# First channel product of the last batch: seven half-size products for eight in each pair of tiles, and the second half of u computed earlier

## The chip, the cores and the metric

The kernel runs on one core of a Trainium2 chip. The metric is the device time of one execution in microseconds; the kernel before has a median of 253.27 us over three runs (252.99 to 253.75). The core's engines are PE (matmuls, with PEld for its weight loads), DVE, ACT and POOL (elementwise work) and SP (which only issues DMAs). Each of them takes its instructions strictly in the order in which they stand in its queue, apart from weight loads on PE, and waits on semaphores for what other engines have to deliver.

## The reference

Attention over a window of 128 positions and 4 sink positions gives x; a residual MLP with affine steps follows. There are 4 batches, 8 heads, 768 positions, 64 elements per head, so x has 512 channels (`DM`), and the inner width `DFF` is 2048.

```python
scores = scale * q @ k.T                 # kept where pos < 4 or 0 <= i - j < 128
x      = softmax(scores) @ v             # heads side by side: 768 x 512 per batch
a1  = alpha1 * x + beta1
tok = w_tok @ a1                         # mixes the 768 positions
u   = x + lam * tok
a2  = alpha2 * u + beta2
out = u + lam * (relu(a2 @ w_ch1) @ w_ch2)
```

The "first channel product" is `a2 @ w_ch1` with its relu, the "second" is `relu(...) @ w_ch2`.

## The kernel before

The work is a list of some thousand tasks. Each task has a function that issues a few instructions on one engine, the tasks it comes after, and the buffers it uses. Nothing is decided while the kernel runs: three tables written into the source give the order in which the tasks are issued (`ORDER`, task numbers), the engine of each (`ENGINES`: 0 ACT, 1 DVE, 2 PE, 3 POOL, 4 SP) and the place of each buffer (`HOMES`). Waits follow from the data and from the reuse of buffers: a task that writes a buffer waits for the last reader of what lay there before.

```python
for i in order:
    t = self.tasks[i]
    e = (ACT, DVE, PE, POOL, SP)[int(engines[i])]
    ...
    t.fn(e)
```

The four batches overlap: while the channel products of batch b run on PE, the attention of batch b+1 is woven in between. The steps that the change touches, with the profile's lines:

- `tok` (L860) multiplies the token weights `wtokT` with `xh`, six tiles of 128 positions per batch (`tok3_0` to `tok3_5` for the last batch), six matmuls each. DVE adds the result to x (L867), giving u; ACT or POOL casts u to half precision (L155, L157); SP issues a transposing DMA for each tile (`uTx`, L919), and an affine step per 128 channels and half of the positions makes a2 transposed, `uT` (L884 on ACT, L886 on DVE).
- `mlp1` (L940) is the first channel product: for each half of the positions (`chk`, 384 of them) and each of 16 tiles of 128 inner channels, four matmuls 128x384 accumulate in one bank of PSUM, and a relu takes it to `hT` in half precision (L946 on ACT, L948 on DVE). In names, `h2_0_7` is batch 2, half 0, tile 7. Per batch that makes 128 matmuls and 32 relus.
- The second channel product of batches 1 to 3 (`prod`, L1057) is done as seven half-size products for eight, P1 to P7, each of three row tiles and eight matmuls 128x256 per tile; P2, P3 and P4 go on top of P1, P5 and P7 in the same banks, and in the names of trace and program they carry those names (a second piece `P5_2_0` is P3). `h_sums` (S1 to S4, L998 to L1001) makes sums and differences of `hT` on DVE in place, `w2_sums` (L972) those of the weights. DVE adds the products to x (L1070, L1088, L1093, L1096; two of the last two kinds also on POOL), after which rows are stored.
- PSUM has four single banks for `h`, `tok` and the P products (kind "d") and two double banks for attention scores (kind "S"). The pieces above therefore take turns in four banks: the next product in a bank waits until DVE or ACT has read what was there.
- In the stretch that the change uses for its new sums (about 150 to 168 us), PE does the last products of batch 1, the first `h2_0_x` tiles of batch 2, and the first scores of batch 3's attention. DVE has x additions, relus and mask multiplications (`E<-E,mask`, L662); POOL has casts of v (`vfs<-vnat`) and a masking select (L587).

```python
a = add(p, {PE: 651}, mm,
        [done["uT", b, chk, c] for c in range(NC)] + [done["w1", fi // 4]],
        [ph, bu])
done["h", b, chk, fi] = add(p + 0.1, {ACT: 395, DVE: 480}, relu, [a], [ph, bh])
```

Of the kernel before, what the change touches and what calls it, by code (L numbers as in the profile page):

```python
# [77 lines left out]
def kernel(  # L78
# [74 lines left out]
    def copy(e, o, i):  # L153
        if e == ACT:
            nc.scalar.copy(o, i)  # L155
        else:
            engine[e].tensor_copy(o, i)  # L157
# [774 lines left out]
    def mlp1(p, b, chk, fi):  # L932
        if fi == 0:
            hT[b, chk] = Buf("hT", None, None, f"hT{b}_{chk}")
        bh, bu = hT[b, chk], uT[b, 0]
        ph = Buf("d", [P, NTOK], FP32, f"h{b}_{chk}_{fi}")

        def mm(e):
            for c in range(NC):
                nc.tensor.matmul(  # L940
                    ph.t, w1f[:, c, fi * P : (fi + 1) * P],
                    bu.t[:, c, chk * NTOK : (chk + 1) * NTOK], start=(c == 0), stop=(c == NC - 1))

        def relu(e):
            if e == ACT:
                nc.scalar.activation(bh.t[:, fi, :], ph.t, AF.Relu)  # L946
            else:
                nc.vector.tensor_scalar_max(bh.t[:, fi, :], ph.t, 0.0)  # L948
# [385 lines left out]
```

## Time and profile before

| what | value |
|---|---|
| median of three runs | 253.27 us (252.99 to 253.75) |
| profiled execution: its own time | 253.3 us |
| profiled execution: span | 251.5 us |
| busy: PE, DVE, ACT, POOL | 245.2, 193.7, 131.5, 107.9 us |
| PE clock granted | 1.00 in every stretch that was read |

The span runs from the first to the last instruction of the profiled execution; 1.8 us of its time lie around the span. Busy time is the time in which an engine had an instruction running. A row of a timeline gives the start, the length, the engine, the source line, the operation, out<-in with buffer names (numbers left out) and shapes, the count xN of instructions drawn together, and in brackets the idle time ahead of it with what ended it.

### The profile page before, as it was taken

The page shows a single profiled execution, that of the slowest core. Times are in us where ns is not written, and L with a number is a line of the kernel's source. Part 1 is how long each engine was busy: PE and PEld are TensorE (multiplying, and loading weights), DVE is VectorE, ACT ScalarE, POOL GpSimd, SP SyncE. Part 2 cuts the span into 40 slices and gives each one's busy share as a digit, 9 for nine tenths or more (in the row PEclk, how much of TensorE's full clock was granted, in tenths as well). Part 3 has the DMA queues.
Part 4 walks back from the last instruction along what each step waited for, and adds up shares of the span by engine and source line. Part 5 has one row for each costly group of instructions (what it writes and reads, how often), then busy time and mean ns, then how long its engine had stood idle before and what let it go on. Part 6 is the DMA issues. An engine that isn't in the chain of part 4 may idle for free.

```text
span 251.5 us, 5513 instructions
## 1 busy us (share of the span) xinstructions
PE 245.2 (98%) x2167; PEld 160.2 (64%) x2167; DVE 193.7 (77%) x401; ACT 131.5 (52%) x218; POOL 107.9 (43%) x126
## 2 busy tenths in 40 slices
PE   8899999999999999999999999999999999999994
PEld 7654655575555444566777676567677676567883
DVE  6898987778788976688889995677689985119883
ACT  2389935788985125687750545556660235543000
POOL 8728724986866516442872040065563130000010
PEclk9999999999999999999999999999999999999999
DMA  6999999999999997796489264420000147100006
GB/s 206 212 262 346 222 183 292 361 357 285 219 208 220 231 198 163 166 257 150 108 171 183 55 148 136 126 65 0 3 0 3 21 77 234 46 0 3 22 3 229
DMA packets 86129, 38.79 MB, mean 154 GB/s; under 512 B 73540, under 2 KB 80460, under 8 KB 86104
## 3 DMA queue, kind: packets, MB, share of 16 engines
q1 hardware_dynamic: 66976, 28.85, 48.2%
q10 hardware_dynamic: 15384, 6.32, 10.5%
q0 software_dynamic: 3744, 3.28, 8.3%
q8 instruction: 17, 0.28, 0.5%
q14 instruction: 8, 0.07, 0.1%
HBM read 29.91 MB, written 6.29 MB: 144 GB/s over the span
## 4 chain that ended last, share of the span: by engine, by line
PE 90%; ACT 4%; DVE 3%; issue 1%; DVEq 0%; ACTq 0%
PE h L940 32%; PE P L1057 22%; PE tok L860 12%; PE ch L1125 8%; PE pv L726 4%; PE S L625 4%; PE idle L148 2%; PE tp L515 1%; ACT wt L822 1%; ACT E L647 1%; DVE qkT L157 1%; PE S L620 1%; PE tp L512 1%; PE pv L719 1%; DVE lb_b L1175 1%
## 5 line engine op out<-in xcount | busy, mean ns | idle before, releaser
L940 PE MATMUL h<-uT,w1f 128*128 128x384 f16 x512 | 89.3, 326 | 0.1
L940 PEld LDWEIGHTS <-w1f 128*128 128x128 f16 x512 | 48.4, 98 | 31.9 <-issue 2.0
L946 ACT ACTIVATE hT<-h 128x384 f16<-128x384 f32 x77 | 36.7, 492 | 34.5 <-PE h L940 30.7
L948 DVE TENSOR_SCALAR hT<-h 128x384 f16<-128x384 f32 x51 | 27.4, 552 | 23.7 <-PE h L940 23.3
L1057 PEld LDWEIGHTS <-hT 128*128 128x128 f16 x408 | 39.3, 98 | 7.2 <-DVE hT L1000 0.7
L647 ACT ACTIVATE E<-S 128x1024 f16<-128x1024 f32 (+1 forms) x39 | 37.9, 1002 | 6.8 <-PE S L625 5.7
L770 POOL TENSOR_TENSOR tm<-x,la_b 128x512 f32<-128x512 f32 x18 | 24.7, 1372 | 22.2 <-DVE xh L773 12.0
L860 PE MATMUL tok<-xh,wtokT 128*128 128x512 f16 x144 | 33.2, 379 | 0.0
L1057 PE MATMUL P<-w2f,hT 128*128 128x256 f16 x216 | 26.8, 273 | 0.0
L155 ACT CAST u<-x 128x512 f16<-128x512 f32 x17 | 10.3, 616 | 28.3 <-DVE x L867 27.3
L1093 POOL TENSOR_TENSOR x<-x,pt 128x256 f32<-128x256 f32 x4 | 3.8, 961 | 46.0 <-DVE pt L1088 46.0
L1070 DVE TENSOR_TENSOR x<-x,P 128x256 f32<-128x256 f32 x45 | 18.0, 417 | 6.8 <-PE P L1057 6.0
L1057 PE MATMUL P<-w2s,hT 128*128 128x256 f16 x192 | 23.3, 273 | 0.0
L860 PEld LDWEIGHTS <-wtokT 128*128 128x128 f16 x144 | 13.8, 98 | 14.8 <-issue 0.2
L1125 PE MATMUL ch<-w2f,hT 128*128 128x512 f16 x96 | 22.7, 379 | 0.0
L752 DVE TENSOR_TENSOR x<-pv,rec 128x256 f32<-128x256 f32 x48 | 20.4, 425 | 1.7
L155 ACT CAST n<-nat 128x768 f16<-128x768 f32 x20 | 16.2, 830 | 7.9 <-DMA out_dram<-x 4.8
L867 DVE TENSOR_TENSOR x<-x,tok 128x512 f32<-128x512 f32 x24 | 16.0, 681 | 4.5 <-PE tok L860 4.3
L726 PEld LDWEIGHTS <-E 128*128 128x128 f16 x328 | 15.2, 97 | 4.9 <-issue 1.1
L726 PE MATMUL pv<-vfs,E 128*128 128x65 f16 x328 | 17.7, 193 | 0.0
L587 POOL TENSOR_SCALAR_AFFINE_SELECT E<-E 128x512 f16<-128x512 f16 x12 | 8.8, 753 | 17.9 <-ACT E L647 17.9
L157 POOL CAST vfs<-vnat 128x512 f16<-128x512 f32 x18 | 13.5, 752 | 4.3 <-PE pv L726 4.2
(133 smaller groups left out, 340.1 us busy)
## 6 DMA issues: line engine op xcount, KB each, us to landing
wst_w<-in_moe_w_ch_dram SPq DMA_DIRECT2D x8, 512.0 KB, 7.4
nat<-in_q_dram SPq DMA_DIRECT2D x10, 384.0 KB, 4.3
nat<-in_k_dram SPq DMA_DIRECT2D x10, 384.0 KB, 8.1
vnat<-in_v_dram SPq DMA_DIRECT2D x14, 256.0 KB, 6.2
out_dram<-x SPq DMA_DIRECT2D x12, 256.0 KB, 3.4
wtn<-in_moe_w_tok_dram SPq DMA_DIRECT2D x6, 384.0 KB, 4.8
out_dram<-x ACTq DMA_DIRECT2D x9, 256.0 KB, 4.3
w1f<-in_moe_w_ch_dram POOLq DMA_DIRECT2D x4, 512.0 KB, 10.2
```

Of the source, the lines that this page charges most:

```text
L155: nc.scalar.copy(o, i)
L647: nc.scalar.activation(eT.t, pS.t[:, :, 0 : n * w].rearrange("p e (i w) -> p e i w", i=n), AF.Exp, scale=scale)
L726: nc.tensor.matmul(po.t[:, hl, :], eT.t[:, e_, off + i, c : c + P], vf[j][:, h, :], start=(r < 2 and n == 0), stop=(n == len(parts) - 1 an ...
L752: nc.vector.tensor_mul(bx.t[:, 4 * G : 4 * G + 4, :], po.t[:, :, 0:D], rec.t.to_broadcast([P, 4, D]))
L770: engine[e].tensor_mul(bt.t, bx.t.rearrange("p h d -> p (h d)"), la1_b)
L860: nc.tensor.matmul(bank(), wtokT[:, si, ti * P : (ti + 1) * P], hs[si].t, start=(si == 0), stop=(si == NR - 1))
L940: nc.tensor.matmul(ph.t, w1f[:, c, fi * P : (fi + 1) * P], bu.t[:, c, chk * NTOK : (chk + 1) * NTOK], start=(c == 0), stop=(c == NC - 1))
L946: nc.scalar.activation(bh.t[:, fi, :], ph.t, AF.Relu)
L948: nc.vector.tensor_scalar_max(bh.t[:, fi, :], ph.t, 0.0)
L1057: nc.tensor.matmul(pc.t, hh[:, nt * P : (nt + 1) * P], w(fi), start=(first and n_ == 0), stop=(n_ == HF - 1), skip_group_check=True)
L1070: nc.vector.tensor_add(row(bx)[:, cols], row(bx)[:, cols], pc.t)
L1125: nc.tensor.matmul(pc.t, bh.t[:, fi, nt * P : (nt + 1) * P], w2f[:, fi, :], start=(fi == 0), stop=(fi == NF - 1))
```

## The change

For batch 3 alone, `mlp1` is replaced by `mlp1_pair`, which is called for i = 0 to 7 and makes inner tiles i and i+8 for both halves of the positions together. The four blocks (two inner tiles by two halves of the positions, with the 512 channels cut in two) are had from seven half-size products P1 to P7 of two matmuls 128x384 each, 14 for the former 16. Three kinds of additions come with it:

- `w1_sums`: sums and differences aS1 to aS4 of quarters of `w_ch1`, each in two halves of 128x2x512 in half precision. They are independent of the data and are placed in the stretch 150 to 168 us, five on POOL and three on DVE.
- `u_sums`: T1 to T4, differences of quarters of `uT` (128x768), T1, T3 and T4 on POOL, T2 on DVE.
- per pair, a copy of P1 from one PSUM bank to another (k1), the relu r11, copies of P6 and P5 to SBUF (k2 and k5, `hU` and `hV`), two additions of a PSUM bank and a copy (a22, a12), the relu r21, and two relus in place in SBUF (`clip`), one on POOL and one on DVE on average: seven passes over PSUM and two clips for the former four passes.

`hA` are the two double banks, which are free of scores by then. For the second half of u, `tok3_3`, `tok3_4` and `tok3_5` are issued ahead of batch 2's products P6, P5 and P3; `tok3_3` and `tok3_4` go to the double banks. The casts, transposes and affine steps behind them move with them.

```diff
-        601, 741, 765, 742, 771, 766, 760, 916, 772, 746, 751, 917, 773, 752, 913, 886,
+        601, 741, 765, 742, 771, 986, 766, 760, 916, 772, 746, 751, 917, 773, 987, 752,
...
-        pt = Buf("S" if (b, ti) == (0, 5) else "d", None, None, f"tok{b}_{ti}")
+        pt = Buf("S" if (b, ti) in ((0, 5), (3, 3), (3, 4)) else "d", None, None, f"tok{b}_{ti}")
...
+    HPAIR = (3,)
+    def w1_sums(p):
+        a11, a12 = w1f[:, 0:2, 0 : DFF // 2], w1f[:, 2:4, 0 : DFF // 2]
+        a21, a22 = w1f[:, 0:2, DFF // 2 : DFF], w1f[:, 2:4, DFF // 2 : DFF]
+        for s in ("S1", "S2", "S3", "S4"):
+            aS[s] = Buf("wst", [P, 2, DFF // 2], FP16, f"w1{s}")
+        for s, sub_, i0, i1, need in (("S1", 0, a21, a22, None), ("S2", 1, "S1", a11, "S1"),
+                                      ("S3", 1, a11, a21, None), ("S4", 1, a12, "S2", "S2")):
+            for g in range(2):
+                f = slice(512 * g, 512 * g + 512)
...
+                    op = engine[e].tensor_sub if sub_ else engine[e].tensor_add
+                    op(aS[s].t[:, :, f], r0[:, :, f], r1[:, :, f])
...
+    def u_sums(p, b):
...
+        for s, i0, i1, need, parts in (("T1", b12, b11, None, c11 + c12), ("T2", b22, "T1", "T1", c22),
+                                       ("T3", b22, b12, None, c12 + c22), ("T4", b21, "T2", "T2", c21)):
...
+                engine[e].tensor_sub(uD[b, s].t, r0, r1)
...
+    def mlp1_pair(p, b, i):
...
+        k_ = i + NF // 2
+        bA = pairs[b, i % 4 // 2]
+        bB = Buf("d", [P, NTOK], FP32, f"hB{b}_{i}")
+        bE = Buf("d", [P, NTOK], FP32, f"hE{b}_{i}")
+        bU = Buf("E", [P, NTOK], FP32, f"hU{b}_{i}")
+        bV = Buf("E", [P, NTOK], FP32, f"hV{b}_{i}")
...
+        m1 = mm("P1", A, lambda n_: w(n_, i), lambda n_: tok_(n_, 0), True, True, w1_ + half, [bA, bu])
+        k1 = add(p, {ACT: 395, DVE: 480}, lambda e, k=f"k1.{i}": copy(e, bB.t, A()), [m1], [bA, bB])
+        m2 = mm("P2", B_, lambda n_: w(2 + n_, i), lambda n_: tok_(2 + n_, 0), False, True, w1_ + half + [k1], [bB, bu])
+        done["h", b, 0, i] = relu("r11", c11, B_, [m2], [bB, h0])
+        m6 = mm("P6", A, lambda n_: sums("S2", n_), lambda n_: uD[b, "T2"].t[:, n_], False, True,
...
+        k2 = add(p, {ACT: 395, DVE: 480}, lambda e, k=f"k2.{i}": copy(e, bU.t, A()), [m6], [bA, bU])
+        m5 = mm("P5", E_, lambda n_: sums("S1", n_), lambda n_: uD[b, "T1"].t[:, n_], True, True,
...
+        m7 = mm("P7", A, lambda n_: sums("S3", n_), lambda n_: uD[b, "T3"].t[:, n_], False, True,
...
+        k5 = add(p, {ACT: 395, DVE: 480}, lambda e, k=f"k5.{i}": copy(e, bV.t, bE.t), [m5], [bE, bV])
+        a22 = plus("a22", c22, A, lambda: bV.t, [m7, k5], [bV, bA, h1])
+        done["h", b, 1, k_] = clip("r22", c22, [a22], [h1])
+        m4 = mm("P4", A, lambda n_: w(2 + n_, k_), lambda n_: uD[b, "T4"].t[:, n_], False, True,
...
+        done["h", b, 0, k_] = relu("r21", c21, A, [m4], [bA, h0])
+        m3 = mm("P3", E_, lambda n_: sums("S4", n_), lambda n_: tok_(2 + n_, 1), False, True,
...
+        a12 = plus("a12", c12, E_, lambda: bU.t, [m3, k2], [bE, bU, h1])
+        done["h", b, 1, i] = clip("r12", c12, [a12], [h1])
...
+        if b in HPAIR:
+            m1 = [("us",)] + [("hp", i) for i in range(NF // 2)]
```

The lines of the functions move: in the changed kernel L981 are the sums of `w_ch1`, L1001 those of `uT`, L1031 the matmuls of a pair, L1044 and L1046 its relus, L1051 the additions, L1056 the clips; L867 is `tok`, L955 DVE's relu of `mlp1`, L669 the mask multiplication, L1202 an addition of a product to x, L1225 and L1228 those from `pt`, L1189 the second channel product.

What the tables do to the queues is seen in the order of the instructions. POOL, at about 150 us, before the change: the last x addition of batch 1 there, a cast of v, the select on batch 3's first scores, more casts.

```order
L1093 TENSOR_TENSOR x1_2_1308<-x1_2_1308,pt1_2_2193 128x256
L157 CAST vfs_98<-vnat3_4_2269 128x8x64
L587 AFFINE_SELECT E3_1_0_2684<-E3_1_0_2684 128x4x128 x2
L157 CAST vfs_98<-vnat3_2_2204 128x8x64
L157 CAST vfs_98<-vnat3_1_2599 128x8x64
```

And in the changed kernel:

```order
L1225 TENSOR_TENSOR x1_2_1308<-x1_2_1308,pt1_2_2193 128x256
L157 CAST vfs_98<-vnat3_4_2269 128x8x64
L981 TENSOR_TENSOR w1S1_2694<-w1f_107 128x2x512
L981 TENSOR_TENSOR w1S2_2696<-w1S1_2694,w1f_107 128x2x512
L981 TENSOR_TENSOR w1S1_2694<-w1f_107 128x2x512
L981 TENSOR_TENSOR w1S2_2696<-w1S1_2694,w1f_107 128x2x512
L981 TENSOR_TENSOR w1S4_2700<-w1f_107,w1S2_2696 128x2x512
L594 AFFINE_SELECT E3_1_0_2687<-E3_1_0_2687 128x4x128 x2
L157 CAST vfs_98<-vnat3_2_2204 128x8x64
```

Five sums now stand between the cast and the select; S2 reads S1, and S4 reads S2, half by half.

DVE in the same stretch, before the change: the last x additions of batch 1 from `pt1` and from the products P5, then the relus of batch 2 with a mask multiplication between.

```order
L1093 TENSOR_TENSOR x1_0_1370<-x1_0_1370,pt1_0_2304 128x256
L1070 TENSOR_TENSOR x1_0_1370<-x1_0_1370,P5_1_0_2496 128x256
L1096 TENSOR_TENSOR x1_4_1530<-x1_4_1530,pt1_1_2181 128x512
L1070 TENSOR_TENSOR x1_4_1530<-x1_4_1530,P5_1_1_2532 128x256
L948 TENSOR_SCALAR hT2_0_2554<-h2_0_7_2559 128x384
L948 TENSOR_SCALAR hT2_0_2554<-h2_0_4_2549 128x384
L948 TENSOR_SCALAR hT2_0_2554<-h2_0_0_2584 128x384
L948 TENSOR_SCALAR hT2_0_2554<-h2_0_11_2591 128x384
L662 TENSOR_TENSOR E3_0_0_2589<-E3_0_0_2589,mask0_80 128x1024
L948 TENSOR_SCALAR hT2_0_2554<-h2_0_5_2601 128x384
```

And in the changed kernel:

```order
L1225 TENSOR_TENSOR x1_0_1370<-x1_0_1370,pt1_0_2304 128x256
L1202 TENSOR_TENSOR x1_0_1370<-x1_0_1370,P5_1_0_2496 128x256
L1228 TENSOR_TENSOR x1_4_1530<-x1_4_1530,pt1_1_2181 128x512
L1202 TENSOR_TENSOR x1_4_1530<-x1_4_1530,P5_1_1_2532 128x256
L981 TENSOR_TENSOR w1S3_2570<-w1f_107 128x2x512
L955 TENSOR_SCALAR hT2_0_2554<-h2_0_7_2559 128x384
L955 TENSOR_SCALAR hT2_0_2554<-h2_0_4_2549 128x384
L981 TENSOR_TENSOR w1S3_2570<-w1f_107 128x2x512
L955 TENSOR_SCALAR hT2_0_2554<-h2_0_0_2586 128x384
L955 TENSOR_SCALAR hT2_0_2554<-h2_0_11_2593 128x384
L669 TENSOR_TENSOR E3_0_0_2591<-E3_0_0_2591,mask0_80 128x1024
L955 TENSOR_SCALAR hT2_0_2554<-h2_0_5_2604 128x384
```

The two halves of S3 stand in front of the relus of `h2_0_7` and `h2_0_0`. (The second half of S4 goes to DVE too, between the relu of `h2_0_15` and the reciprocal `rec3_0_0`, some dozen rows later.) In this stretch everything else has kept its order on both engines.

PE, the first matmul of each group from `tok3_2` on (at about 195 us), before the change:

```order
L860 MATMUL tok3_2_3193<-xh3_0_2832,wtokT_106 128x512
L1057 MATMUL P6_2_0_3201<-w2s0_1491,hT2_0_2554 128x256
L1057 MATMUL P6_2_1_3228<-w2s0_1491,hT2_0_2554 128x256
L860 MATMUL tok3_4_3240<-xh3_0_2832,wtokT_106 128x512
L860 MATMUL tok3_3_3250<-xh3_0_2832,wtokT_106 128x512
L1057 MATMUL P5_2_0_3263<-w2s0_1491,hT2_1_2884 128x256
L860 MATMUL tok3_5_3273<-xh3_0_2832,wtokT_106 128x512
L940 MATMUL h3_0_1_3333<-uT3_3237,w1f_107 128x384
```

And in the changed kernel, up to the second product that uses a T sum:

```order
L867 MATMUL tok3_2_3204<-xh3_0_2844,wtokT_106 128x512
L867 MATMUL tok3_3_3216<-xh3_0_2844,wtokT_106 128x512
L867 MATMUL tok3_4_3228<-xh3_0_2844,wtokT_106 128x512
L867 MATMUL tok3_5_3240<-xh3_0_2844,wtokT_106 128x512
L1189 MATMUL P6_2_1_3254<-w2s0_1491,hT2_0_2554 128x256
L1189 MATMUL P6_2_2_3264<-w2s0_1491,hT2_0_2554 128x256
L1031 MATMUL hA3_1_3305<-uT3_3213,w1f_107 128x384
L1031 MATMUL hB3_0_3322<-uT3_3213,w1f_107 128x384
L1031 MATMUL hE3_0_3390<-uD3T1_3344,w1S1_2694 128x384
L1031 MATMUL hB3_1_3375<-uT3_3213,w1f_107 128x384
L1031 MATMUL hA3_0_3309<-uD3T2_3373,w1S2_2696 128x384
```

The token products `tok3_3` to `tok3_5` have moved ahead of P6 of batch 2, and where `h3_0_1` opened the first channel product, products of the pairs stand between batch 2's last products, first those that need no sum. Ahead of `tok3_3` PE's queue is unchanged.

More of the change, by code (lines that the diff above doesn't have):

```diff
@@ L953, in mlp1, with f_ @@
         done["h", b, chk, fi] = add(p + 0.1, {ACT: 395, DVE: 480}, relu, [a], [ph, bh])
+    HPAIR = (3,)
+    aS = {}
+    uD = {}
+    pairs = {}
+    def w1_sums(p):
[7 more added lines that the diff above has]
+                f = slice(512 * g, 512 * g + 512)
+                def f_(e, s=s, sub_=sub_, i0=i0, i1=i1, f=f):
+                    r0, r1 = [aS[z].t if isinstance(z, str) else z for z in (i0, i1)]
+                    op = engine[e].tensor_sub if sub_ else engine[e].tensor_add
+                    op(aS[s].t[:, :, f], r0[:, :, f], r1[:, :, f])
+                done["a" + s, g] = add(
+                    p, {POOL: 2500, DVE: 700}, f_,
+                    [done["w1", i] for i in range(4)] + ([done["a" + need, g]] if need else []),
+                    [aS[s]] + ([aS[need]] if need else []), port=True)
@@ new lines, in mlp1_pair, with mm, f_, tok_ @@
+    def mlp1_pair(p, b, i):
+        bu = uT[b, 0]
+        if i == 0:
+            for chk in range(2):
+                hT[b, chk] = Buf("hT", None, None, f"hT{b}_{chk}")
+            for g in range(2):
+                pairs[b, g] = Buf("S", None, None, f"hA{b}_{g}")
+        h0, h1 = hT[b, 0], hT[b, 1]
+        k_ = i + NF // 2
[4 more added lines that the diff above has]
+        bV = Buf("E", [P, NTOK], FP32, f"hV{b}_{i}")
+        A = lambda: bA.t[:, i % 2, 0:NTOK]
+        w = lambda c, f: w1f[:, c, f * P : (f + 1) * P]
+        g = i // 4
+        def mm(name, o, ws, xs, start, stop, after, uses):
+            def f_(e, name=f"{name}.{i}"):
+                for n_ in range(2):
+                    nc.tensor.matmul(o(), ws(n_), xs(n_), start=start and n_ == 0, stop=n_ == 1,
+                                     skip_group_check=True)
+            return add(p, {PE: 326}, f_, after, uses)
+        def tok_(c, chk):
+            return bu.t[:, c, chk * NTOK : (chk + 1) * NTOK]
+        def sums(s, n_):
+            return aS[s].t[:, n_, i * P : (i + 1) * P]
+        def relu(name, o, pt, after, uses):
+            def f_(e, name=f"{name}.{i}"):
+                if e == ACT:
+                    nc.scalar.activation(o(), pt(), AF.Relu)
+                else:
+                    nc.vector.tensor_scalar_max(o(), pt(), 0.0)
+            return add(p, {ACT: 395, DVE: 480}, f_, after, uses)
+        def plus(name, o, i0, i1, after, uses):
+            def f_(e, name=f"{name}.{i}"):
+                nc.vector.tensor_add(o(), i0(), i1())
+            return add(p, {DVE: 480}, f_, after, uses)
+        def clip(name, o, after, uses):
+            def f_(e, name=f"{name}.{i}"):
+                engine[e].tensor_scalar_max(o(), o(), 0.0)
+            return add(p, {POOL: 600, DVE: 250}, f_, after, uses, port=True)
+        w1_ = [done["w1", z] for z in range(4)]
+        B_ = lambda: bB.t
+        E_ = lambda: bE.t
+        c11, c21 = (lambda: h0.t[:, i, :]), (lambda: h0.t[:, k_, :])
+        c12, c22 = (lambda: h1.t[:, i, :]), (lambda: h1.t[:, k_, :])
+        half = [done["uT", b, 0, c] for c in range(NC)]
+        m1 = mm("P1", A, lambda n_: w(n_, i), lambda n_: tok_(n_, 0), True, True, w1_ + half, [bA, bu])
[3 more added lines that the diff above has]
+        m6 = mm("P6", A, lambda n_: sums("S2", n_), lambda n_: uD[b, "T2"].t[:, n_], False, True,
+                [k1, done["aS2", g], done["uT2", b]], [bA, aS["S2"], uD[b, "T2"]])
+        k2 = add(p, {ACT: 395, DVE: 480}, lambda e, k=f"k2.{i}": copy(e, bU.t, A()), [m6], [bA, bU])
+        m5 = mm("P5", E_, lambda n_: sums("S1", n_), lambda n_: uD[b, "T1"].t[:, n_], True, True,
+                [done["aS1", g], done["uT1", b]], [bE, aS["S1"], uD[b, "T1"]])
+        m7 = mm("P7", A, lambda n_: sums("S3", n_), lambda n_: uD[b, "T3"].t[:, n_], False, True,
+                [k2, done["aS3", g], done["uT3", b]], [bA, aS["S3"], uD[b, "T3"]])
+        k5 = add(p, {ACT: 395, DVE: 480}, lambda e, k=f"k5.{i}": copy(e, bV.t, bE.t), [m5], [bE, bV])
+        a22 = plus("a22", c22, A, lambda: bV.t, [m7, k5], [bV, bA, h1])
+        done["h", b, 1, k_] = clip("r22", c22, [a22], [h1])
+        m4 = mm("P4", A, lambda n_: w(2 + n_, k_), lambda n_: uD[b, "T4"].t[:, n_], False, True,
+                w1_ + [a22, done["uT4", b]], [bA, uD[b, "T4"]])
+        done["h", b, 0, k_] = relu("r21", c21, A, [m4], [bA, h0])
+        m3 = mm("P3", E_, lambda n_: sums("S4", n_), lambda n_: tok_(2 + n_, 1), False, True,
+                [k5, done["aS4", g]] + [done["uT", b, 1, c] for c in range(NC)], [bE, aS["S4"], bu])
+        a12 = plus("a12", c12, E_, lambda: bU.t, [m3, k2], [bE, bU, h1])
+        done["h", b, 1, i] = clip("r12", c12, [a12], [h1])
@@ L1230 @@
             seq += two("P1", "P2")
-            i = seq.index(("m1", 1, 8))
+            i = seq.index(("pr", "P1", 0) if b in HPAIR else ("m1", 1, 8))
             seq[i:i] = [("hs", "S3")]
@@ L1261 @@
                 p -= PAR["p7"]
-            {"tok": tok, "uT": uTp, "m1": mlp1, "m2": mlp2, "hs": h_sums, "pr": prod}[what](p, b, *args)
+            {"tok": tok, "uT": uTp, "m1": mlp1, "m2": mlp2, "hs": h_sums, "pr": prod,
+             "us": u_sums, "hp": mlp1_pair}[what](p, b, *args)
             if b and what == "tok":
```

26 lines of the change are left out of this document (21 added, 5 removed), and 56 rows, old and new, of the table ORDER.

## The prediction

> **What bounds the kernel now.** I read the engine totals first, then the chain of waits, then the busy time by stretches, and last the timelines of the engines around the places where the change puts work.
>
> ```profile
> span 251.5 us, 5513 instructions
> PE 245.2 (98%) x2167; PEld 160.2 (64%) x2167; DVE 193.7 (77%) x401; ACT 131.5 (52%) x218; POOL 107.9 (43%) x126
> PE 90%; ACT 4%; DVE 3%; issue 1%; DVEq 0%; ACTq 0%
> L940 PE MATMUL h<-uT,w1f 128*128 128x384 f16 x512 | 89.3, 326 | 0.1
> 152.26 2.60 PE h L940 x16
> ...
> 155.40 4.66 PE h L940 x28
> ...
> 210.10 18.85 PE h L940 x116
> 228.95 1.75 PE P L1057 x16
> ...
> 247.98 0.42 DVE x L1070
> ```
>
> PE is busy for 245.2 of 251.5 us, and 90% of the chain that ended last is PE's. The chain's own rows give the real pace: 116 first-product matmuls in 18.85 us are 0.1625 us each (the 326 ns of the group row is a length with overlap).
>
> ```profile
> 150.00:155.00 5.00, 5.00 (x40) 3.43 (x39) 3.25 (x8) 1.19 (x3) 0.43 (x1) 1.00 0.48 166
> 155.00:160.00 5.00, 5.00 (x38) 2.78 (x35) 3.98 (x8) 2.62 (x5) 0.00 (x0) 1.00 0.68 175
> ...
> 215.00:220.00 5.00, 5.00 (x32) 3.01 (x31) 0.56 (x1) 3.40 (x9) 0.00 (x0) 1.00 0.14 52
> 220.00:225.00 5.00, 5.00 (x33) 3.03 (x31) 1.12 (x2) 2.61 (x6) 0.00 (x0) 1.00 0.00 0
> ```
>
> After the stretch come busy PE, weight loads, DVE, ACT and POOL, then PE's granted clock. PE is busy 5.00 of 5 us both where the weight sums go (150 to 165) and where the pairs go (215 to 225), at a clock of 1.00. So a matmul taken away is worth its full time, and a wait put on PE costs its full time too. Between those ends the other engines look free: POOL did nothing from 155 to 160.
>
> **Part 1: fewer matmuls.** 128 become 112, so 16 × 0.1625 = 2.6 us less on the path. That is certain as PE work; only waits can eat it. **−2.6.**
>
> **Part 2: five weight sums on POOL.** They fill this hole:
>
> ```profile
> 149.80 0.64 POOL L157 CAST vfs<-vnat 128x512 f16<-128x512 f32 x1
> 163.86 1.22 POOL L587 TENSOR_SCALAR_AFFINE_SELECT E<-E 128x512 f16<-128x512 f16 x2 [13.43 <-ACT E L647]
> ...
> 96.25 1.16 POOL L972 TENSOR_TENSOR w2s<-w2f,w2s 128x512 f16<-128x512 f16 x1
> 97.36 1.16 POOL L972 TENSOR_TENSOR w2f<-w2f 128x512 f16<-128x512 f16 x1
> ```
>
> Two sums of half the size start 1.11 us apart, so one of 1024 elements per partition takes about 2.15 us (2 × 1.16 = 2.32 above, and less if part of 1.16 is fixed). Five are 10.8 us, and the hole is 13.43. Counted by POOL alone they cost nothing. [...]
>
> But other rows show what a running POOL instruction does to DVE.
>
> ```profile
> 97.75 1.32 DVE L662 TENSOR_TENSOR E<-E,mask 128x1024 f16<-128x1024 f16 x1
> 157.31 0.68 DVE L662 TENSOR_TENSOR E<-E,mask 128x1024 f16<-128x1024 f16 x1
> 189.49 1.27 POOL L770 TENSOR_TENSOR tm<-x,la_b 128x512 f32<-128x512 f32 x1
> 189.85 1.72 DVE L999 TENSOR_TENSOR hT<-hT 128x1536 f16<-128x1536 f16 x1
> 185.99 0.95 DVE L998 TENSOR_TENSOR hS<-hT,hT 128x1536 f16<-128x1536 f16 x1
> 186.22 1.84 POOL L770 TENSOR_TENSOR tm<-x,la_b 128x512 f32<-128x512 f32 x1 [0.50 <-DVE x L752]
> 42.70 5.40 POOL L839 TENSOR_TENSOR w2f<-wst_w,lam_b 128x512 f16<-128x512 f32 x4
> 44.53 1.22 DVE L839 TENSOR_TENSOR w2f<-wst_w,lam_b 128x512 f16<-128x512 f32 x1
> ```
>
> The mask multiplication takes 0.68 us with POOL idle and 1.32 when it starts 0.39 us into POOL's sum of 97.36; it ends at 99.07, which is POOL's end (98.52) plus 0.55. The same with `hT`: 1.72 for 0.95, ending 0.81 after POOL's 190.76. It goes the other way too: POOL's `tm` of 186.22 takes 1.84 for 1.27, since DVE's `hS` ran to 186.94. So a DVE operation with two inputs in SBUF stands still until POOL's running instruction ends, and POOL's next waits for it. Operations that read PSUM (relus, additions of a product) do not show it. In the row of 42.70 POOL has four in a row and DVE gets in after the one that was running, so I take turns: DVE waits for the rest of one sum, not for all five. [...]
>
> DVE's queue while the sums would run:
>
> ```profile
> 150.83 0.42 DVE L1093 TENSOR_TENSOR x<-x,pt 128x256 f32<-128x256 f32 x1
> 151.42 0.42 DVE L1070 TENSOR_TENSOR x<-x,P 128x256 f32<-128x256 f32 x1 [0.17 <-PE P L1057]
> 151.76 0.68 DVE L1096 TENSOR_TENSOR x<-x,pt 128x512 f32<-128x512 f32 x1
> 152.55 0.42 DVE L1070 TENSOR_TENSOR x<-x,P 128x256 f32<-128x256 f32 x1
> 154.24 1.02 DVE L948 TENSOR_SCALAR hT<-h 128x384 f16<-128x384 f32 x2 [1.27 <-PE h L940]
> 156.19 1.21 DVE L948 TENSOR_SCALAR hT<-h 128x384 f16<-128x384 f32 x2 [0.93 <-PE h L940]
> 157.91 1.48 DVE L948 TENSOR_SCALAR hT<-h 128x384 f16<-128x384 f32 x3
> ```
>
> Five instructions there read SBUF twice: L1093, L1096, the two halves of S3 that the change adds (1024 elements, 0.6 us by L662's 0.68), and the mask at 157.31. Each meets a different sum. POOL's first starts at 150.44, after its cast. The walk, in the time of before:
>
> - The addition of 150.83 waits for sum 1 (to 152.6), ends 152.9; the L1070 behind it frees a bank at 153.3. The tile `h2_0_3` took that bank from 152.26 on (the chain's row): PE waits about 1.3.
> - Sum 2 runs 152.9 to 155.1; L1096 waits for it, to 155.7.
> - Sum 3 runs 155.7 to 157.85; S3's first half waits, to 158.5. The relu of `h2_0_7` behind it ends at 159.0. Its bank is the next `h2_0_0` needs, which started at 155.40: PE is now 3.6 late.
> - Sum 4 runs 158.5 to 160.6; S3's second half waits, to 161.2; relu of `h2_0_0` to 161.7 (PE 4.5 late).
> - Sum 5 runs 161.2 to 163.35; the mask waits, to 163.95; the relu of `h2_0_5` ends at 164.4. Before it was the first of the three from 157.91, so it started 0.47 apart and its bank was free for `h2_0_13` at about 158.6. PE is 5.8 late.
>
> As a sum: five POOL sums 10.75, DVE's 0.33 + 0.6 + 0.6 + 0.6 between them, mask and relu 1.05, from 150.44 to 164.4, against 158.6. Lower bound: nothing, if DVE is not held (then it only pays its own S3, 1.2 us into idle time of 1.27 and 0.93). Upper bound: DVE gets no turn until all five are done (150.44 + 10.75 = 161.2, against 150.83: about 10 late). Between them I take 5.8, since four rows show the hold and the row of 44.53 shows the turn.
>
> The second half of S4 on DVE stands between a relu and `rec3_0_0`, beside POOL's casts of v:
>
> ```profile
> 165.03 1.17 POOL L157 CAST vfs<-vnat 128x512 f16<-128x512 f32 x2
> 165.32 0.56 DVE L948 TENSOR_SCALAR hT<-h 128x384 f16<-128x384 f32 x1 [0.55 <-PE h L940]
> 165.79 0.17 DVE L751 RECIPROCAL rec<-pv 128x4 f32<-128x4 f32 x1
> ```
>
> It pushes the reciprocal and the x behind it by 0.6, or by 1.2 if it meets a cast; a bank of PE hangs on them. Bounds 0.3 and 1.2, taken 0.8. Part 2 together: **+6.6.**
>
> **Part 3: tokens ahead.** `tok3_3` to `tok3_5` change places with P6, P5 and P3 pieces; the amount of PE work is the same, and the double banks they use have no scores left. Six transposes on SP then follow earlier tokens:
>
> ```profile
> 199.02 9.28 SPq L919 DMA_TRANSPOSE uT<-u  x6
> 206.03 0.60 ACT L155 CAST u<-x 128x512 f16<-128x512 f32 x1
> ```
>
> The last cast, at 206.03 before, comes to about 202, and u is whole near 206.5, about 3.6 us ahead of the first product with a T sum (tokens end at 200.7; then 24 + 24 second-product pieces, 10 matmuls of pairs and 24 pieces: 210.1). What covers it are these pieces. Taken as 0, between −0.3 and +0.5.
>
> **Part 4: the pairs.** Each makes seven passes over PSUM for four, 56 for 32, and 16 clips, in 112 × 0.1625 = 18.2 us. DVE's share is 27 passes and 8 clips, ACT's 29 passes.
>
> ```profile
> L948 DVE TENSOR_SCALAR hT<-h 128x384 f16<-128x384 f32 x51 | 27.4, 552 | 23.7 <-PE h L940 23.3
> L946 ACT ACTIVATE hT<-h 128x384 f16<-128x384 f32 x77 | 36.7, 492 | 34.5 <-PE h L940 30.7
> L998 DVE TENSOR_TENSOR hS<-hT,hT 128x1536 f16<-128x1536 f16 x6 | 6.6, 1109 | 0.5 <-ACT hT L946 0.3
> ```
>
> Back to back a relu starts every 0.46 to 0.5 us (three in 1.48), so DVE has 27 × 0.48 + 8 × 0.3 + two `hS`-like sums 1.9 = 17.3 us in 18.2, where the rows 215 to 225 gave it 1.68 in 10. ACT has some 13. DVE is nearly full but not the bound, as long as it is fed evenly; PE's four single and two double banks then wait now and then. T2 (DVE) reads T1 and meets T3 on POOL, 768 elements, 1.6 us: T1 is done at about 208.7, T3 at 210.3, T2 at 210.9, and the product with T2 is due at 210.8, so up to 0.75. A k1 copy that comes late behind it, 0.5; uneven feeding, some 0.75 more. Bounds: 0 (all covered) and +4 (DVE at 0.55 per pass is 19.2 us, 1.0 over, and three or four such waits). I take **+2.0**. The tail from P1 on is as before and takes nothing.
>
> **Sum.** −2.6 + 6.6 + 0 + 2.0 = +6.0 on a span of 251.5, 257.5; with the 1.8 us around it (253.3 − 251.5) 259.3. The profiled run's 253.3 stands at the median, 253.27. I forecast 259.3 us, slower.
>
> **Rivals.**
>
> *The sums hide in POOL's hole (faster).* If a wide POOL sum leaves DVE its turns without holding it, or if the five start much later than 150.44, so that DVE is already ahead, part 2 shrinks to about 0.3. For it: the hole of 13.43 us is longer than the 10.8, and in the stretches DVE has idle time (5 − 3.25, 5 − 3.98). Against it: the four stretched rows. It decides where the hold costs PE less than 2.6 − 2.0 = 0.6 us. Time: 253.3 − 2.6 + 0.3 + 1.3 (part 4 without DVE's late start) = 252.3, between 251 and 253.7.
>
> *DVE gets no turn (much slower).* POOL's next sum may start before DVE's waiting instruction does; sums 2, 4 and 5 wait only for POOL itself. PE then waits once, near 10 us for `h2_0_3`, and nothing afterwards: 253.3 − 2.6 + 10 + 0.8 + 2.0 = 263.5. For it: nothing holds POOL back by semaphore. Against it: 44.53, where DVE got in. [...]
>
> *DVE becomes the bound in the pairs.* If passes take 0.55 us and every bank waits, part 4 is +4 or more and the time 261.3, on top of part 2; without part 2's hold, 255.
>
> **How the numbers follow.** 0.3%, 0.76 us, is about what a measurement of this kernel can tell from no change. The hold with turns: 0.68 (256.5 to 262, from part 2 between 4 and 8 and part 4 between 1 and 4). Hidden: 0.20, of which 0.15 is faster by over 0.3% and 0.05 within it. No turns: 0.08. DVE the bound without the hold: 0.04, slower by a little. So faster 0.16, same 0.06, slower 0.78. The range reaches down to 252.8, for most of the sum's lower cases, and up to 263.5, leaving about 0.2 outside; the likeliest case's own is 256.5 to 262.
>
> **What would show it.** In the changed kernel's timeline, five L981 rows on POOL of about 2.2 us, from about 150.4, some longer by DVE's turn; on DVE, L1225, L1228, the two L981 and the first L669 with lengths of 1.2 to 2.8 us; PE idle by some 6 us between 152 and 165, ended by DVE's x and `hT`. Wrong would be L669 at 0.68 beside a running sum, or PE at 5.00 in those stretches. PE's busy time should fall by 2.6. In the pairs, DVE at 90% or more, and PE's idle time about 2 us, ended by DVE; above 4 would overturn part 4, and PE late by less than 0.6 before 170 the forecast's sign.

## The result and the profile after

The changed kernel takes 261.78 us (median of four runs, 261.45 to 262.18) against 253.27, a ratio of 1.034 with a 95% interval of 1.0321 to 1.0358: 8.5 us slower. The forecast was 259.3, with 263.5 as the upper end of its range. The profiled execution took 261.45 us with a span of 259.6, 8.1 more than the span before. Its page, in the lines that answer to those of before:

```profile
span 259.6 us, 5563 instructions
PE 245.0 (94%) x2151; PEld 158.9 (61%) x2151; DVE 214.3 (83%) x430; ACT 134.0 (52%) x224; POOL 135.7 (52%) x143
PE 75%; DVE 11%; ACT 4%; DMA 3%; POOL 3%; issue 2%; DVEq 0%; POOLq 0%; ACTq 0%
```

PE falls from 90% of the last chain to 75%, and DVE comes up from 3% to 11%. PE's busy time is 245.0 us for 245.2, although it has 16 matmuls less (2151 for 2167): a row of two matmuls lasts 0.48 us while the next can start 0.32 after it, so a matmul's record reaches some 0.16 us into a wait. PE therefore shows less idle time than it loses, and the delays below are taken from when each matmul starts.

The stretches where the weight sums went, and two of the pairs' stage (columns as before: PE, PEld, DVE, ACT, POOL, clock):

```profile
150.00:155.00 5.00, 3.66 (x32) 2.84 (x31) 4.21 (x6) 0.13 (x1) 4.92 (x4) 1.00 0.51 147
155.00:160.00 5.00, 3.32 (x26) 1.88 (x25) 4.89 (x6) 3.27 (x7) 4.92 (x3) 1.00 0.29 80
160.00:165.00 5.00, 3.50 (x22) 1.88 (x21) 5.00 (x7) 0.44 (x1) 3.26 (x2) 1.00 0.64 184
...
215.00:220.00 5.00, 4.33 (x36) 3.21 (x34) 4.63 (x8) 2.28 (x7) 3.96 (x3) 1.00 0.57 206
220.00:225.00 5.00, 4.11 (x25) 2.25 (x24) 3.60 (x8) 2.04 (x5) 2.60 (x3) 1.00 0.11 41
```

Before the change PE was at 5.00 in all of these stretches. From 150 to 165 DVE now looks full (4.21, 4.89, 5.00), but with 19 instructions for the 22 of before. The timelines of POOL and DVE side by side tell why:

```profile
151.28 2.12 POOL L981 TENSOR_TENSOR w1S<-w1f 128x1024 f16<-128x1024 f16 x1
153.48 2.19 POOL L981 TENSOR_TENSOR w1S<-w1S,w1f 128x1024 f16<-128x1024 f16 x1
155.63 2.57 POOL L981 TENSOR_TENSOR w1S<-w1f 128x1024 f16<-128x1024 f16 x1
158.28 2.46 POOL L981 TENSOR_TENSOR w1S<-w1S,w1f 128x1024 f16<-128x1024 f16 x1
160.69 2.57 POOL L981 TENSOR_TENSOR w1S<-w1f,w1S 128x1024 f16<-128x1024 f16 x1
```

```profile
151.63 2.06 DVE L1225 TENSOR_TENSOR x<-x,pt 128x256 f32<-128x256 f32 x1
153.79 0.42 DVE L1202 TENSOR_TENSOR x<-x,P 128x256 f32<-128x256 f32 x1
154.13 2.08 DVE L1228 TENSOR_TENSOR x<-x,pt 128x512 f32<-128x512 f32 x1
156.32 0.42 DVE L1202 TENSOR_TENSOR x<-x,P 128x256 f32<-128x256 f32 x1
156.66 2.09 DVE L981 TENSOR_TENSOR w1S<-w1f 128x1024 f16<-128x1024 f16 x1
158.67 1.01 DVE L955 TENSOR_SCALAR hT<-h 128x384 f16<-128x384 f32 x2
159.60 1.68 DVE L981 TENSOR_TENSOR w1S<-w1f 128x1024 f16<-128x1024 f16 x1
161.20 1.01 DVE L955 TENSOR_SCALAR hT<-h 128x384 f16<-128x384 f32 x2
162.13 1.68 DVE L669 TENSOR_TENSOR E<-E,mask 128x1024 f16<-128x1024 f16 x1
```

Both engines' rows start in the order of their queues. So do PE's matmuls in the traces of before and after (2167 and 2151), while 197 and 196 of its weight loads start up to 0.11 us ahead of the matmul in front of them.

Each of DVE's five instructions with two inputs in SBUF ends a few tenths after one of POOL's sums (the first at 153.69, POOL's at 153.40; the other four 0.54 or 0.55 after theirs), and takes 1.7 to 2.1 us for 0.42 to 0.68. The L1202, which read a product from PSUM, keep their 0.42 (the same additions before, L1070 on DVE, took 0.41 to 0.42 each, all 45). What PE waited for from 148 to 176 (instruction, what released it, us in total, times, longest):

```profile
PE h L947 <- DVE hT L955: 3.2, 3, 1.7
PE h L947 <- DVE x L1202: 1.3, 1, 1.3
PE h L947 <- DVE x L759: 0.7, 1, 0.7
```

Set against the same matmuls of the trace before, PE is later by 0.8 us at 150 already, by 2.2 at `h2_0_3`, 3.9 at `h2_0_0`, 4.5 at `h2_0_8`, 5.75 at `h2_0_13` and 6.6 at `h2_0_9`. So 5.8 us arise between 150 and 173, and 1.5 after that (8.1 − 0.8 − 5.8), where 2.6 us of matmuls were saved: the pairs' stage has some 4.1 us of waits. Of the 0.8, some 0.65 arise in the first 18 us, in code that is alike (PE's first 67 filler matmuls took 5.40 us for 5.15, then transposes waited for input). This start differs from execution to execution: at 20 us into the span, PE stands between 0.05 us earlier and 1.2 us later than in the trace before in the traces below.

### The profile page after: what moved, and what is told of

Its sections match the earlier page's. It is cut to its first block, busy times and chain, and to the rows that moved or that the text cites. A ratio compares the mean times of both kernels' runs of the same rounds, so it can differ in the third digit from the quotient of the medians.

```text
span 259.6 us, 5563 instructions
## 1 busy us (share of the span) xinstructions
PE 245.0 (94%) x2151; PEld 158.9 (61%) x2151; DVE 214.3 (83%) x430; ACT 134.0 (52%) x224; POOL 135.7 (52%) x143
## 4 chain that ended last, share of the span: by engine, by line
PE 75%; DVE 11%; ACT 4%; DMA 3%; POOL 3%; issue 2%; DVEq 0%; POOLq 0%; ACTq 0%
PE h L947 21%; PE P L1189 20%; PE tok L867 12%; PE ch L1257 8%; PE pv L733 3%; DMA n<-in_q_dram 3%; PE S L632 3%; PE hA L1031 2%; DVE w1S L981 2%; DVE x L1228 2%; DVE hT L1051 2%; ACT wt L829 1%; PE hE L1031 1%; ACT E L654 1%; DVE hT L955 1%
## 5 line engine op out<-in xcount | busy, mean ns | idle before, releaser
L947 PE MATMUL h<-uT,w1f 128*128 128x384 f16 x384 | 68.4, 326 | 5.3 <-DVE hT L955 3.2
L947 PEld LDWEIGHTS <-w1f 128*128 128x128 f16 x384 | 35.9, 98 | 30.0 <-issue 5.6
L1189 PEld LDWEIGHTS <-hT 128*128 128x128 f16 x408 | 39.4, 98 | 6.7 <-DVE hT L1132 0.3
L953 ACT ACTIVATE hT<-h 128x384 f16<-128x384 f32 x55 | 26.4, 492 | 26.7 <-PE h L947 26.5
L867 PE MATMUL tok<-xh,wtokT 128*128 128x512 f16 x144 | 32.8, 379 | 0.0
L955 DVE TENSOR_SCALAR hT<-h 128x384 f16<-128x384 f32 x41 | 21.8, 550 | 8.9 <-PE h L947 8.8
L1189 PE MATMUL P<-w2f,hT 128*128 128x256 f16 x216 | 26.4, 273 | 0.0
L1202 DVE TENSOR_TENSOR x<-x,P 128x256 f32<-128x256 f32 x45 | 18.2, 415 | 6.1 <-PE P L1189 5.7
L867 PEld LDWEIGHTS <-wtokT 128*128 128x128 f16 x144 | 13.8, 98 | 15.2 <-issue 0.2
L1189 PE MATMUL P<-w2s,hT 128*128 128x256 f16 x192 | 22.9, 272 | 0.0
L157 POOL CAST u<-x 128x512 f16<-128x512 f32 x7 | 4.6, 657 | 26.5 <-DVE x L874 17.8
L1056 POOL TENSOR_SCALAR hT<-hT 128x384 f16<-128x384 f16 x8 | 9.3, 1176 | 11.2 <-DVE hT L1051 11.2
```

What stands on the lines that cost most here:

```text
L867: nc.tensor.matmul(bank(), wtokT[:, si, ti * P : (ti + 1) * P], hs[si].t, start=(si == 0), stop=(si == NR - 1))
L947: nc.tensor.matmul(ph.t, w1f[:, c, fi * P : (fi + 1) * P], bu.t[:, c, chk * NTOK : (chk + 1) * NTOK], start=(c == 0), stop=(c == NC - 1))
L1189: nc.tensor.matmul(pc.t, hh[:, nt * P : (nt + 1) * P], w(fi), start=(first and n_ == 0), stop=(n_ == HF - 1), skip_group_check=True)
```

## Experiments

The theory: the hold of DVE by POOL's sums costs about 5.8 us, and waits between the pairs' own passes the rest. The rivals were that the sums hide and the pairs cost everything, and that DVE is simply full.

**The sums alone.** The kernel before with the eight sums of `w_ch1` added at the same places of both queues, unread.

```diff
+    w1_sums(0)        # tasks put into ORDER behind the same neighbours, same engines
     plan.emit(ORDER, ENGINES, HOMES, IDLES)
```

> The kernel before with nothing but the eight sums of w_ch1 added, in the same places of POOL's and DVE's queues; nothing reads them. Theory (a DVE instruction with two inputs in SBUF stands still while a POOL sum runs, and PE waits behind DVE): PE is 5.8 us late by 175 us, as in the changed kernel, and the time is 253.3 + 5.8 = 259.1 us (258 to 260). Rival (the sums hide in POOL's hole, and the changed kernel lost its time elsewhere): 253.3 to 254 us.

Measured: 259.94 us (259.41 to 259.98) beside 253.94 for the kernel before on the same chip, ratio 1.0236 (1.0205 to 1.0267), 6.0 us. PE's waits of 148 to 176:

```profile
PE h L940 <- DVE hT L948: 3.2, 3, 1.7
PE h L940 <- DVE x L1070: 1.3, 1, 1.3
PE h L940 <- DVE x L752: 0.8, 1, 0.8
```

They are those of the changed kernel to a tenth. So 6.0 of the 8.5 us come with sums that POOL has idle time for, and nothing of the pairs is needed for them. The last of the three waits (0.8) does not come from POOL's five sums: it stands behind the second half of S4, which DVE makes itself.

**The pairs alone.** The changed kernel with quarters of `w_ch1` in place of the sums (its first product of batch 3 is therefore made from other numbers), and no sums computed.

```diff
-            return aS[s].t[:, n_, i * P : (i + 1) * P]
+            c0, f0 = {"S1": (2, 0), "S2": (0, 0), "S3": (0, DFF // 2), "S4": (2, DFF // 2)}[s]
+            return w1f[:, c0 + n_, f0 + i * P : f0 + (i + 1) * P]
...
-            w1_sums(w0 - 50)
```

> The changed kernel without the eight sums: plain quarters of w_ch1 stand in their place, so the first product of batch 3 is computed from other numbers, with the same matmuls, passes and T sums. Theory: only the 5.8 us before 175 go, so 261.8 - 5.8 = 256.0 us, still above the kernel before, since the pairs lose about 4 us of waits against the 2.6 us that they save. Rival (the late start of the pairs' stage is what makes its waits, so with DVE in time they shrink to 2 us or less): 254 us or less.

Measured: 255.77 us (255.21 to 256.61) beside 253.94, ratio 1.0071 (1.0047 to 1.0096): 1.8 us slower than before. PE's waits in the pairs' stage are those of the changed kernel (1.3 for `hB`, 0.9 and 0.5 for `hT`), though it starts 6 us earlier, so the late start does not make them. The two parts come to 6.0 + 1.8 = 7.8 of the 8.5 us. By the 0.7 that is left the two medians of the kernel before differ, 253.27 beside the changed kernel and 253.94 here. PE also runs without a gap from `tok3_3` to 206 us in this trace, so the tokens put ahead cost nothing.

**Narrower sums on POOL.**

```diff
-                    op(aS[s].t[:, :, f], r0[:, :, f], r1[:, :, f])
+                    k = 128 if e == POOL else 512
+                    for q_ in range(f.start, f.stop, k):
+                        w_ = slice(q_, q_ + k)
+                        op(aS[s].t[:, :, w_], r0[:, :, w_], r1[:, :, w_])
```

> The changed kernel with each of POOL's five sums of w_ch1 cut into four instructions of a quarter of the width; the same elements in all. Theory (the hold lasts for one POOL instruction): each held DVE instruction waits 0.6 us at most in place of 1.0 to 1.8, PE is some 2 to 3 us late by 175 us instead of 5.8, and the time is 258.3 to 259.3 us. Rival (POOL and DVE share a path, and DVE is slowed in proportion to POOL's busy time): no gain, 261.5 to 262.5 us, a little more for the longer POOL time.

Measured: 256.89 us (256.62 to 257.38), ratio 1.0123 (1.0091 to 1.0154). Of the 6.0 us only 1.1 is left (256.89 − 255.77), less than either theory said, although POOL is now busy for longer:

```profile
150.63 3.73 POOL L982 TENSOR_TENSOR w1S<-w1f 128x256 f16<-128x256 f16 x4
154.32 2.99 POOL L982 TENSOR_TENSOR w1S<-w1S,w1f 128x256 f16<-128x256 f16 x4
...
150.97 0.60 DVE L1226 TENSOR_TENSOR x<-x,pt 128x256 f32<-128x256 f32 x1
152.01 0.69 DVE L1229 TENSOR_TENSOR x<-x,pt 128x512 f32<-128x512 f32 x1
153.14 0.69 DVE L982 TENSOR_TENSOR w1S<-w1f 128x1024 f16<-128x1024 f16 x1
```

The hold lasted for the rest of one POOL instruction: beside pieces of 0.75 to 0.93 us a DVE instruction waited a few tenths (0.60 us for 0.42, 1.10 for the mask's 0.68), which DVE's idle time took up. A path shared in proportion would have shown no gain. Of PE's waits that are left from 148 to 176, the longest (0.8) is again the one behind DVE's own half of S4; POOL's pieces account for two of 0.2.

**All sums on DVE**, one or two at a time where DVE waited for PE before.

```diff
     # engine of tasks 982 to 985 and 988 (S1, S2 and the first half of S4)
-    POOL
+    DVE, ahead of: the relu of h2_0_2 (both S1), x2_2 <- P1 (both S2), rec3_3_0 and rec3_5_1 (S4)
```

> The changed kernel with POOL's five sums of w_ch1 given to DVE, and the eight halves put one or two at a time where DVE waited for PE in the kernel before (about 153, 155, 160, 175, 178 and 187 us). Theory: DVE does each in 0.65 us, mostly in its own idle time, nothing holds it, and PE is at most 1 us late by 190 us: 256 to 257 us. Rival (DVE has no time left, and any sum on it costs PE its length): 8 x 0.65 = 5.2 us late, 261 us.

Measured: 256.31 us (256.06 to 256.45), ratio 1.0097 (1.0067 to 1.0126). The eight sums cost 0.5 us beside the kernel without them (256.31 − 255.77), by the trace all of it at 191 and 193 us, behind the last one, which pushed DVE's queue:

```profile
160.71 1.28 DVE L979 TENSOR_TENSOR w1S<-w1f 128x1024 f16<-128x1024 f16 x2
...
191.34 2.82 PE L1187 MATMUL P<-w2s,hT 128*128 128x256 f16 x23 [0.19 <-DVE x L1200]
```

DVE took 0.64 to 0.69 us each for five of the sums, and 2.11 for the two at 175.75, where POOL took 2.1 to 2.6 for one. DVE was not out of time.

**Which POOL instructions hold DVE.** The kernel before with the additions of the first experiment, but POOL's five made to read nothing, or to read once.

```diff
-                    op(aS[s].t[:, :, f], r0[:, :, f], r1[:, :, f])
+                    if e == POOL:
+                        nc.gpsimd.memset(aS[s].t, 0.0)                                     # one kernel
+                        nc.gpsimd.tensor_copy(aS[s].t, w1f[:, 0:2, 0 : DFF // 2])          # the other
+                    else:
+                        op(aS[s].t[:, :, f], r0[:, :, f], r1[:, :, f])
```

> The kernel before with the eight instructions of the first experiment in the same places, but POOL's five write zeros (memset, 2048 elements per partition each, 1.5 to 2.5 us) and read nothing; DVE's three sums stay. Nothing reads the results. Theory in its narrow form (POOL holds DVE only where both need to read SBUF through the same path): PE is late by DVE's own three sums at most, under 1 us, 253.3 to 254.5 us. Rival (any running POOL instruction holds a DVE instruction with two inputs in SBUF): some 6 us late in proportion to the lengths, 258 to 260 us.

> The same with POOL's five instructions as copies with one input in SBUF (2048 elements of half precision per partition, 2.0 to 2.6 us each). Theory: a POOL instruction that reads SBUF once holds DVE as one that reads twice does: 5 to 7 us late, 258.5 to 260.5 us. Rival (only POOL's second input takes the path that DVE needs): as with the memsets, 253.3 to 254.5 us.

Measured: with memsets 254.13 us (253.62 to 255.21), ratio 1.0018 (1.0001 to 1.0034); with copies 258.20 (257.89 to 258.8), ratio 1.0176 (1.0153 to 1.0200); 253.76 for the kernel before. First the memsets, then the copies, each with DVE beside them:

```profile
151.19 8.78 POOL L1315 MEMSET w1S<- 128x2048 f16 x5
...
151.65 0.42 DVE L1093 TENSOR_TENSOR x<-x,pt 128x256 f32<-128x256 f32 x1
152.58 0.69 DVE L1096 TENSOR_TENSOR x<-x,pt 128x512 f32<-128x512 f32 x1
158.13 0.68 DVE L662 TENSOR_TENSOR E<-E,mask 128x1024 f16<-128x1024 f16 x1
```

```profile
151.64 10.80 POOL L1315 COPY w1S<-w1f 128x2048 f16<-128x2048 f16 x5
...
152.00 1.80 DVE L1093 TENSOR_TENSOR x<-x,pt 128x256 f32<-128x256 f32 x1
154.25 1.85 DVE L1096 TENSOR_TENSOR x<-x,pt 128x512 f32<-128x512 f32 x1
161.54 1.44 DVE L662 TENSOR_TENSOR E<-E,mask 128x1024 f16<-128x1024 f16 x1
```

Beside 8.78 us of memsets these DVE instructions take what they take alone (0.42, 0.69 and 0.68 us for 0.42, 0.68 and 0.68), and PE's only wait from 148 to 176 is the 0.8 behind DVE's half of S4. Beside copies that read SBUF once, they stand still as beside sums (1.80 for 0.42, 1.85 and 1.44 for 0.68). That much of the narrow form the two runs show: POOL's copies, which read SBUF, held DVE, and its memsets, which read nothing, did not. A path that both need was not shown. The copies cost 4.4 us (258.20 − 253.76) where the sums cost 6.0: five of them took 10.80 us with DVE's turns, about 2.2 us each, where the sums had 2.1 to 2.6.

**The pairs in another order.** The kernel with all sums on DVE, the same instructions, with seven tasks on another engine and 17 moved by 1 to 12 places; and the same with the seven changes of engine alone.

```diff
     # engine                                             # place in the order, among others
-    T1: POOL      x2_5 <- pt: DVE    one r21: ACT       T2, the sums S1 of hT and S4: 3 to 6 places later or earlier
+    T1: DVE       x2_5 <- pt: POOL   one r21: DVE       products of pairs 0 to 2 (P3, P5, P6): 2 to 9 places
-    hU of pair 2, hB of pair 5: DVE   two clips: one DVE, one POOL
+    hU of pair 2, hB of pair 5: ACT   two clips: exchanged
```

> The kernel of the experiment with all sums on DVE, with the same instructions in the same number, but 17 tasks after 186 us in another place of the order and seven of them on another engine (T1 and one relu to DVE, two copies from DVE to ACT, one x addition to POOL, two clips exchanged). Theory (the waits in the pairs' stage come from the order: PE waits for a reader of the other half of a double bank that stands late in DVE's or ACT's queue): PE's waits after 195 us fall from 4.7 us to under 1.5, and the time from 256.3 to 252.5 to 253.3 us, at or a little below the kernel before. Rival (DVE is full in that stage and sets its length whatever the order): no more than 0.5 us less, 255.8 us or above.

> Only the seven changes of engine of that kernel, with every task in its old place of the order. Theory: some of the waits go, since the instructions behind the moved ones come earlier; about half of the gain, 253.8 to 255 us. Rival (DVE's load decides): as the seven changes leave DVE's number of passes nearly as it was (four tasks away, three to it), no gain, 256 us or above.

Measured: 252.03 us (251.50 to 254.14) with both, ratio to before 0.9946 (0.9922 to 0.9970); 254.54 (253.69 to 255.24) with the engines alone, ratio 1.0031 (1.0014 to 1.0048); 253.76 for the kernel before. The first is faster than both kernels, by 1.7 and by some 10 us. (Ten of its twelve runs lie between 251.50 and 252.89 and two at 254.1; what sets those two apart stays open.) PE's waits from 195 to 236 us, first with the engines alone, then with both, where one is left. The two rows behind them give the busy time of PE, PEld, DVE, ACT and POOL from the first to the last matmul of the pairs, first in the changed kernel, then with both:

```profile
PE hA L1029 <- DVE hB L157: 0.5, 1, 0.5
PE hA L1029 <- DVE hT L1049: 0.5, 1, 0.5
PE hA L1029 <- DVE hT L1044: 0.5, 1, 0.5
...
PE hA L1029 <- ACT hT L1042: 0.3, 1, 0.3
...
210.63:238.10 27.47, 24.63 (x161) 15.41 (x159) 23.05 (x47) 12.84 (x29) 14.30 (x12) 1.00 0.18 63
204.04:228.10 24.06, 23.81 (x161) 15.45 (x159) 20.30 (x46) 13.49 (x30) 13.78 (x12) 1.00 0.21 72
```

Summed over consecutive matmuls (how much later than its usual distance each started), PE's delay after 186 us is 4.7 us with all sums on DVE (4.2 of it after 195), 2.9 with the engines changed as well, and 0.8 with both. Between the last two kernels only the order differs: 2.5 us. DVE's share of the stage is the same in the best kernel as in the changed one (20.30 of 24.06 and 23.05 of 27.47 us, both 84%), though the stage is 3.4 us shorter. So a full DVE is not what set the stage's length. The new order was not tried without the changes of engine.

Where the 4.1 us of the changed kernel arose is seen there, in rows of PE, DVE, ACT and POOL:

```profile
209.59 2.24 POOL L1225 TENSOR_TENSOR x<-x,pt 128x256 f32<-128x256 f32 x2 [0.70 <-DVE pt L1220]
210.36 2.02 DVE L1228 TENSOR_TENSOR x<-x,pt 128x512 f32<-128x512 f32 x2
212.30 0.55 DVE L157 COPY hB<-hA 128x384 f32<-128x384 f32 x1
212.91 0.48 PE L1031 MATMUL hA<-uT,w1f 128*128 128x384 f16 x2 [0.59 <-DVE hB L157]
...
223.61 0.48 ACT L155 COPY hU<-hA 128x384 f32<-128x384 f32 x1 [0.84 <-DVE hT L1051]
223.99 0.50 ACT L1044 ACTIVATE hT<-hA 128x384 f16<-128x384 f32 x1
224.54 0.48 PE L1031 MATMUL hA<-uD3T,w1f 128*128 128x384 f16 x2 [0.89 <-ACT hT L1044]
```

The first wait is the hold again: two additions on POOL (2.24 us, for 0.72 each alone) and two on DVE (2.02 for 1.3) stand in each other's way, the copy `hB` comes late behind them, and PE behind it. The second is a queue: ACT's relu, for which PE waits, stands behind a copy that waits for DVE. In both, the product that waits writes one half of a double bank and the pass it waits for reads the other half (pair 1 and the copy of pair 0; pair 0 and the relu of pair 1, by the names in the order): the double bank is one buffer in the program, so two pairs wait for each other's readers. The second product shows it best: the last reader of its own half, an addition on DVE, had ended at 222.77, and the product started only at 224.54, behind the relu. That this coupling costs the time, apart from the order, was not tried on its own.

## Why the prediction was right, point by point

**The hold, and its turns, were right.** The main case forecast that each of five DVE instructions meets another sum and gets its turn behind it; the two timelines above show just that. The walk gave PE 1.3 late at `h2_0_3`, 3.6, 4.5 and 5.8 at the three that follow; measured (without the 0.8 of the start) 1.4, 3.15, 3.7 and 5.0. The term was taken 0.8 too high. The five sums began where they were expected, but took 11.98 us from the first's start to the last's end, where the walk has 12.9: it gave each DVE instruction between two sums its 0.33 or 0.6 in full, while POOL's next sum was 0.3 to 0.45 longer for it (2.46 to 2.57 us for 2.12), and the second hardly at all (2.19). The second half of S4 was taken at 0.8 and cost 0.8. The step that predicted from the row of 44.53 that DVE gets in between POOL's instructions decided between 259 and 263.5, and it held: none of the five DVE instructions waited for two sums.

**The tokens ahead** were taken as 0 and cost 0, seen in the kernel without sums.

**The pairs: the term was mis-sized, and most of its waits were not the ones named.** −2.6 was right: PE's delay in that stage, 4.1 us, minus 2.6 gives the 1.5 that the spans differ by. But the waits were these 4.1 us, where I took 2.0, and by the forecast's own sign (above 4 overturns this part) the part does not stand. Of the two waits that I named, one came: T2 was held by T3 (1.66 us, where the kernel with the new order took 0.74 for it), and the copy `hB` behind it made PE 0.83 late, where I had put 0.5 on such a copy and 0.75 on the product that reads T2, which did not wait. "Uneven feeding, some 0.75" was the term that failed. The rest, 3.3 us, falls under it: 0.75 for a copy `hB` behind additions to x that POOL held, a hold that I had not seen coming, then 1.05, 0.65, 0.3, 0.2 and smaller ones. I had sized the term by DVE's load, and expected DVE at 90% or more; it was at 4.63, 3.60, 3.50 and 4.51 of 5 us from 215 to 235, 81%. Load is not what makes these waits. Where a pass stands in the queues is, as the last two kernels show: with the same share of DVE busy they fall from 4.7 to 2.9 us by seven changes of engine, and to 0.8 by the order.

**The start** of 0.8 us in the profiled execution was in no term; it belongs to the execution, not to the change: the traces of the experiments start up to 1.2 us later than the one before, with the same code there.

The errors, 0.8 too much in the hold, 2.1 too little in the pairs and 0.8 at the start, leave 2.1 of the 2.5 us by which the forecast fell short (the rest is the other runs' distance from the profiled one). That it fell short by no more has some luck in it, since the hold's error ran against the other two.

**The rivals.** The sums did not hide: the kernel with the sums alone lost 6.0 us. DVE got its turns (none of the five waited for two sums, and PE's longest wait there was 1.7 us), so the 10 us of waiting in one piece did not come. PE's granted clock was 1.00 in the traces of before and after, so a lower clock is no part of the loss. DVE as the bound of the pairs is refuted by the new order.

## What to carry to other kernels

An idle engine is not free time: before work is given to POOL, look at which DVE instructions beside it read SBUF twice, because each of the five waited here for the POOL instruction in progress (1.7 to 2.1 us for 0.42 to 0.68), and what hung behind DVE's queue waited too (PE for up to 1.7 us). Where it has to be POOL, cut the instruction (with pieces of 0.75 us the sums cost 1.1 us instead of 6.0), or let it only write (0.42 us for 0.42 beside memsets); where DVE has idle time, give DVE the work (0.5 us). And where a saving on the bound engine is paid with more passes on others, judge it by where those passes stand in the queues, not by their load: the same instructions on the same engines gave 254.5 us in one order and 252.0 in another.

## What the runs showed of the hardware that was not expected

POOL's memsets, which only write SBUF, did not touch DVE's additions at all: five memsets in 8.78 us beside DVE rows of unchanged length (0.42 and 0.69 us for 0.42 and 0.68). Cutting a sum in four lengthens POOL's time from 2.12 to 2.99 us, but what the kernel loses by the sums shrinks from 6.0 to 1.1 us: DVE's additions take 0.60 and 0.69 us instead of 2.06 and 2.08, and idle time of DVE covers waits that short.

Two inputs in SBUF are not the whole condition. DVE's affine step on `uT` (L893) reads one tensor, with a factor and an offset from `ab`. It started at 214.64 in the changed kernel, while POOL made T1 (213.93 to 215.58), took 1.05 us for 0.37 and ended at 215.70. Nor is the turn certain: in the trace with the memsets such a step started at 149.84, when an addition on POOL had 0.14 us to go, and POOL's next addition (149.95 to 150.67) went ahead of it; the step took 0.95 us.

POOL's clips (one input, in place) fit neither way. Two of them beside one of DVE's in the changed kernel, and one of them beside another:

```profile
233.89 2.29 POOL L1056 TENSOR_SCALAR hT<-hT 128x384 f16<-128x384 f16 x2 [3.86 <-DVE hT L1051]
235.12 0.52 DVE L1056 TENSOR_SCALAR hT<-hT 128x384 f16<-128x384 f16 x1
...
223.56 1.15 POOL L1056 TENSOR_SCALAR hT<-hT 128x384 f16<-128x384 f16 x1
223.96 0.25 DVE L1056 TENSOR_SCALAR hT<-hT 128x384 f16<-128x384 f16 x1
```

The first of DVE's clips takes 0.52 us for 0.25 alone, but ends at 235.64, while POOL's second clip runs until 236.18. The second lies wholly within a clip of POOL's and is not longer than alone. Why this kind of instruction is held for less, or not at all, was not tried and stays open.
